# The threshold of an assignment by binary search, spread to all partitions by VectorE instead of by a matmul

## The chip, the cores and the metric

One core of a Trainium2 chip. The metric is the device time of one execution in microseconds (us): 890.03 us for the kernel before, the median of 3 runs (889.72 to 890.83).

## What is computed

Attention with a window of 128 keys, then two products with a leaky ReLU between them, then a mixture of 8 experts in which each token goes to one expert:

```python
def _moe2_ref(x, w_gate, w1, w2):
    cap = N // E
    flat = (x @ w_gate).flatten()
    order = np.argsort(-flat)
    for idx in order:
        tok, e = (int(idx) // E, int(idx) % E)
        if assigned[tok] >= 0 or counts[e] >= cap:
            continue
        assigned[tok] = e
        counts[e] += 1
    for e in range(E):
        mask = assigned == e
        out[mask] = np.maximum(x[mask] @ w1[e], 0.0) @ w2[e]
```

2304 tokens, 8 experts, 288 places each. The tokens are assigned greedily in the order of their logits over all experts. The change lies in this assignment.

## The kernel before

Products in fp32 are made of three: operands are split into a high and a low part, and high x high, high x low, low x high are summed. The high part is ScalarE's (a copy into a narrower type), the low part VectorE's (the difference).

The stages follow one another: attention with the first product (`w_in`), the second product (`w_out`, to `x2_dram`), and the experts. The second product has 18 blocks of 128 tokens, each of 48 matmuls of 512 columns into one bank `po` (line 221). It is written as a generator: `fill(n)` emits the next n of these matmuls wherever it is called. The order on every engine is the order of the code in this part.

The assignment (`assign`, line 744 on) needs the logits alone and runs beside the second product. It has 7 phases. In each, every open token names the expert that it likes best, and a search finds, for all experts at once, a threshold above which the tokens fit into the places left. The search has two calls of `search` with three rounds each, so 42 rounds in all: the first two rounds of a call try 32 values, the third 64. One round is:

- VectorE compares the keys with the values: `ge` (line 805; 128x576 for 32 values, 128x1152 for 64), and subtracts the last threshold from the keys (line 806);
- `low()` takes a low part from a list (line 808, the work at line 189): a piece of 128x512 of a block of the second product to come or of an expert's weight;
- TensorE does 6 or 9 fills (`F_GE`), then 18 small matmuls that count, per value and expert, the keys that pass: `cnt` (line 812), 32 or 64 rows;
- VectorE reads the counts (`jk`, `mx`, line 815) and tests whether they fill a place: `ok` (line 818), one number per value, on 32 or 64 partitions;
- if the list holds more than 2 pieces, a second low part (line 820);
- TensorE does 3 fills (`F_NB`) and a matmul of ones by `ok`, which sums `ok` and leaves the threshold on all 128 partitions of a PSUM bank, `nb` (line 823). The next comparison reads it as its scalar.

At the end of a phase, totals go through TensorE (`tp`, lines 741 to 871). Behind the last phase stand 22 fills, a prefix sum by TensorE (`pre`), a chain on VectorE (`t`, `w`, `W`, `U`, lines 900 to 920), 24 fills and the matmuls `ip` (line 924) that give the list of tokens of each expert. What is left in the list of low parts is done behind that (line 940), unless a block needs it: the generator calls `lows_of` ahead of a block's first and 25th matmul, which emits the missing low parts there.

A low part's second piece also issues, on SP's queue, the load that reuses its buffer (`gin`, line 201); ScalarE makes the high part of that load (`goh`, line 181).

Of the kernel before, what the change touches and what calls it, by code (L numbers as in the profile page):

```python
# [9 lines left out]
F32 = mybir.dt.float32  # L10
F32R = mybir.dt.float32r
BF16 = mybir.dt.bfloat16
# [3 lines left out]
ALU = mybir.AluOpType  # L16
AX = mybir.AxisListType.X
PSUM = bass.MemoryType.PSUM

P = 128  # L20
# [26 lines left out]
LOW_PIECES = 2  # L47
# [77 lines left out]
def tile_attn_moe_moe2(ctx: ExitStack, tc: tile.TileContext, q_in, k_in, v, w_in, w_out, w_gate, w1, w2, consts, out):  # L125
    nc = tc.nc
    V, A, T, GP = nc.vector, nc.scalar, nc.tensor, nc.gpsimd
# [9 lines left out]
    def bank(tag, name, bufs=None):  # L137
        kw = {} if bufs is None else dict(bufs=bufs)
        return ps.tile([P, 512], F32, tag=tag, name=name, **kw)
# [4 lines left out]
    def C(name):  # L144
        return cst[:, COLS[name][0]:COLS[name][1]]
# [3 lines left out]
    ones_b = cpool.tile([P, P], BF16, name="ones_b")  # L149
# [27 lines left out]
    lows = []  # L177
# [8 lines left out]
    def low(n=1):  # L186
        for _ in range(min(n, len(lows))):
            wl, cs, st, wh, then = lows.pop(0)
            V.tensor_tensor(out=wl[:, cs], in0=st[:, cs], in1=wh[:, cs].bitcast(F32), op=ALU.subtract)  # L189
            if then:  # L190
                then()
# [48 lines left out]
    def fill(n):  # L240

        nonlocal emitted
        for _ in range(n):
            emitted += next(products, 0) is None
# [56 lines left out]
    with ExitStack() as actx:  # L301
# [283 lines left out]
        if True:  # L585
# [13 lines left out]
            for c in range(H // 2):  # L599
                (V if c < BIAS_V else GP).tensor_scalar(bias_sb[:, c, :], C("rel"), C("slope")[:, c:c + 1], None,  # L600
                                                        op0=ALU.mult)
# [120 lines left out]
    def rt(shape, dt, tag, bufs=1):  # L722
        return bpool.tile(shape, dt, tag=tag, name=tag, bufs=bufs)

    def TT(o, a, b, op):
        V.tensor_tensor(out=o, in0=a, in1=b, op=op)
# [13 lines left out]
    def prefix_sum(src, acc, pre):  # L740
        T.matmul(pre, tri_b, src.rearrange("p e i -> p i e"), start=True, stop=False)
        T.matmul(pre[:, 1:], ones_b, acc[:, :, :NB - 1].rearrange("p e i -> p i e"), start=False, stop=True)

    def assign(fill):
# [5 lines left out]
                        op1=ALU.bitwise_or)  # L750
# [46 lines left out]
        def search(kt, nb, oh, weight, beside):  # L797

            for cn, n, step in (("c1", 32, 2048.0), ("c2", 32, 64.0), ("c3", 64, weight)):
                ge = rt([P, NB, n], BF16, f"ge{n}")  # L800
                k, c = kt.unsqueeze(2).to_broadcast([P, NB, n]), C(cn).unsqueeze(1).to_broadcast([P, NB, n])
                if nb is None:
                    TT(ge, k, c, ALU.is_ge)
                else:
                    V.scalar_tensor_tensor(out=ge, in0=k, scalar=nb, in1=c, op0=ALU.subtract, op1=ALU.is_ge)
                    V.tensor_scalar(kt, kt, nb, None, op0=ALU.subtract)
                beside[cn]()
                low()
                fill(F_GE[n])
                cnt = bank("t", "cnt")[:n, :NE]  # L810
                for i in range(NB):
                    T.matmul(cnt, ge[:, i, :], oh[:, i, :], start=(i == 0), stop=(i == NB - 1))  # L812
                jk = rt([P, NE], F32, "jk")
                mx = rt([P, 1], F32, "mx")
                V.tensor_tensor_reduce(out=jk[:n], in0=cnt, in1=need[:n], scale=1.0, scalar=-1e9,
                                       op0=ALU.subtract, op1=ALU.max, accum_out=mx[:n])
                ok = rt([P, 1], BF16, "ok")
                V.tensor_scalar(ok[:n], mx[:n], 0.0, step, op0=ALU.is_ge, op1=ALU.mult)
                if len(lows) > LOW_PIECES:
                    low()  # L820
                fill(F_NB)
                nb = bank("v", "nb", bufs=1)[:, :1]
                T.matmul(nb, ones_b[:n, :], ok[:n], start=True, stop=True)
            return nb

        for ph in range(NE - 1):
# [21 lines left out]
            def nothing():  # L848
                pass

            nb = search(kh, None, oh, 65536.0, dict(c1=low_key, c2=account, c3=both_keys))
            nb = search(k2, nb, oh, 1.0, dict(c1=nothing, c2=nothing, c3=nothing))

            m1, m0 = rt([P, NB], F32, "m1"), rt([P, NB], F32, "m0")
# [8 lines left out]
            with nc.allow_low_precision("counts up to 18"):  # L863
# [23 lines left out]
                                   op1=ALU.add)  # L887
# [5 lines left out]
        TT(ab, asg, oh, ALU.add)  # L893

        fill(F_PRE)
        pre = bank("l", "pre", bufs=1)[:, :NB * NE].rearrange("p (i e) -> p i e", i=NB)
        prefix_sum(ab_e, acc, pre)
        t1, t2 = rt(B3, F32, "t1"), rt(B3, F32, "t2")
# [24 lines left out]
        for i in range(NB):  # L923
            T.matmul(ip, U[:, i, :], W[:, i].rearrange("p a c -> p (a c)"), start=(i == 0),
                     stop=(i == NB - 1))
# [3 lines left out]
                               op1=ALU.add)  # L929
# [7 lines left out]
        first["hot"] = hot.rearrange("p g s -> p (g s)")  # L937

    assign(fill)
    low(len(lows))  # L940
    fill((NB - 1) * 48 + 1 - emitted)
# [172 lines left out]
```

## Time and profile before

| | |
|---|---|
| median of 3 runs | 890.03 us (889.72 to 890.83) |
| the profiled execution | 894.0 us, its span 892.2 us |
| TensorE matmuls, share of the span | 839.7 us, 94% |
| VectorE, share of the span | 523.0 us, 59% |
| ScalarE, share of the span | 394.1 us, 44% |
| matmuls of the second product (line 221) in the chain that ended last | 23% of the span |
| counts (line 812) in that chain | 3% of the span |

The chain that ended last is followed back from the last instruction to whatever released each step; 81% of it is TensorE, 8% VectorE, 5% ScalarE. The assignment lies between about 400 and 616 us of the span. A busy time is that of an engine's instructions from start to end, and neighbours on one engine can overlap.

### The profile page before, as it was taken

How to read it: one execution, taken by the hardware profiler on the slowest of the kernel's cores; microseconds unless marked ns; L12 is line 12 of the kernel's file. 1: busy time of each engine (PE TensorE's matmuls, PEld its weight loads, DVE VectorE, ACT ScalarE, POOL GpSimd, SP SyncE). 2: the span in 40 equal slices, each digit the busy share in tenths (PEclk: the TensorE clock that was granted, in tenths of full speed). 3: DMA queues.
4: the chain of work that ended last, by engine and by line, in shares of the span. 5: the costliest groups of instructions: out<-in, count | busy, mean ns of one | idle time of the engine just before them, and what ended most of it. 6: DMA issues, size and time to landing. Idle time of an engine off the chain costs nothing.

```text
span 892.2 us, 18599 instructions
## 1 busy us (share of the span) xinstructions
PE 839.7 (94%) x7590; PEld 732.4 (82%) x7590; DVE 523.0 (59%) x1311; ACT 394.1 (44%) x867; POOL 56.4 (6%) x82
## 2 busy tenths in 40 slices
PE   5578899899999999999999999998999999999995
PEld 3467889899999888877776767776889999999995
DVE  3778774767744452358778787774235555555540
ACT  6776665565655553232121212111234655556551
POOL 0000000000000000000000000000020222112211
PEclk9788899899999999999999999999999999999998
DMA  9964665765539998763324242221345665566630
GB/s 293 250 225 152 186 200 182 207 185 172 172 96 238 246 241 215 189 191 122 133 73 143 85 140 84 95 83 69 121 136 166 214 191 174 181 211 212 189 111 27
DMA packets 103638, 147.19 MB, mean 165 GB/s; under 512 B 6145, under 2 KB 74369, under 8 KB 101505
## 3 DMA queue, kind: packets, MB, share of 16 engines
q1 hardware_dynamic: 100480, 136.56, 51.2%
q0 software_dynamic: 3072, 9.44, 3.1%
q8 instruction: 60, 0.98, 0.5%
q14 instruction: 26, 0.20, 0.1%
HBM read 113.21 MB, written 32.77 MB: 164 GB/s over the span
## 4 chain that ended last, share of the span: by engine, by line
PE 81%; DVE 8%; ACT 5%; issue 4%; POOL 1%; DMA 0%; SPq 0%; POOLq 0%; ACTq 0%; DVEq 0%
PE po L221 23%; PE h L507 21%; PE m L992 11%; PE y L1011 10%; PE xv L482 3%; PE pt L465 3%; PE cnt L812 3%; PE lg L534 2%; PE s L423 2%; ACT pr L453 2%; ACT pr L441 2%; DVE dt L361 1%; PE wtp L386 1%; PE yo L1021 1%; ACT dt L343 1%
## 5 line engine op out<-in xcount | busy, mean ns | idle before, releaser
L221 PE MATMUL po<-wh_out,gol 128*128 128x512 f32 x272 | 112.0, 412 | 4.6 <-DVE gol L189 4.6
L221 PE MATMUL po<-wh_out,goh 128*128 128x512 f32 x272 | 110.6, 406 | 0.0
L221 PE MATMUL po<-wl_out,goh 128*128 128x512 f32 x272 | 110.5, 406 | 0.0
L507 PE MATMUL h<-xh,wh_in 128*128 128x256 f32 x576 | 96.7, 292 | 4.1 <-DVE gb L520 4.1
L520 DVE TENSOR_TENSOR gb<-h,th 128x512 f32<-128x512 f32 x72 | 49.7, 690 | 80.6 <-ACT th L516 77.1
L181 ACT ACTIVATE goh<-gin 128x1024 fp32r<-128x1024 f32 x34 | 36.0, 1060 | 126.9 <-DMA gin<-g_dram 120.9
L507 PE MATMUL h<-xh,wl_in 128*128 128x256 f32 x576 | 91.2, 281 | 0.0
L507 PE MATMUL h<-xl,wh_in 128*128 128x256 f32 x576 | 90.6, 280 | 0.0
L516 ACT ACTIVATE th<-h 128x512 f32<-128x512 f32 x72 | 42.7, 594 | 107.5 <-PE h L507 107.5
L158 DVE TENSOR_TENSOR wl_w<-st_w,wh_w 128x1024 fp32r<-128x1024 f32 x60 | 72.9, 1225 | 26.7 <-ACT wh_w L157 26.7
L507 PEld LDWEIGHTS h<-xh,wh_in 128*128 128x128 f32 x576 | 80.3, 196 | 9.1 <-DVE gb L520 4.5
L507 PEld LDWEIGHTS h<-xh,wl_in 128*128 128x128 f32 x576 | 78.9, 193 | 0.0
L507 PEld LDWEIGHTS h<-xl,wh_in 128*128 128x128 f32 x576 | 77.7, 190 | 0.0
L1011 PE MATMUL y<-hh,wh_w 128*128 128x288 f32 x256 | 77.4, 302 | 0.0
L1011 PE MATMUL y<-hh,wl_w 128*128 128x288 f32 x256 | 75.6, 295 | 0.0
L1011 PE MATMUL y<-hl,wh_w 128*128 128x288 f32 x256 | 75.5, 295 | 0.0
L441 ACT ACTIVATE pr<-neg,nm 128x192 f32<-128x192 f32 (+2 forms) x144 | 61.2, 428 | 29.5 <-DVE nm L438 29.2
L221 PEld LDWEIGHTS po<-wh_out,gol 128*128 128x128 f32 x272 | 51.5, 189 | 15.9 <-DVE gol L189 6.3
L157 ACT ACTIVATE wh_w<-st_w 128x1024 fp32r<-128x1024 f32 x60 | 62.5, 1053 | 2.8 <-DMA st_w<-in_w_dram 2.8
L221 PEld LDWEIGHTS po<-wl_out,goh 128*128 128x128 f32 x272 | 51.4, 189 | 10.1 <-issue 0.2
L995 DVE SCALAR_TENSOR_TENSOR hl<-m,hh 128x288 fp32r<-128x288 f32 x64 | 29.1, 455 | 51.8 <-ACT hh L994 51.8
L221 PEld LDWEIGHTS po<-wh_out,goh 128*128 128x128 f32 x272 | 51.5, 190 | 9.5
(219 smaller groups left out, 1541.0 us busy)
## 6 DMA issues: line engine op xcount, KB each, us to landing
st_w<-in_w_dram SPq DMA_DIRECT2D x64, 512.0 KB, 4.0
g_dram<-gb SPq DMA_DIRECT2D x72, 256.0 KB, 3.9
gin<-g_dram SPq DMA_DIRECT2D x34, 512.0 KB, 3.9
gr<-g_dram SPq DMA_DIRECT2D x48, 256.0 KB, 6.1
v<-in_v_dram SPq DMA_DIRECT2D x28, 384.0 KB, 5.8
raw<-in_w_in_dram SPq DMA_DIRECT2D x8, 1024.0 KB, 9.5
raw<-in_w_out_dram SPq DMA_DIRECT2D x8, 1024.0 KB, 5.4
x_dram<-xo SPq DMA_DIRECT2D x17, 256.0 KB, 2.0
```

Of the source, the lines that this page charges most:

```text
L157: A.activation(wh, st, AF.Copy)
L158: lo_engine.tensor_tensor(out=wl, in0=st, in1=wh.bitcast(F32), op=ALU.subtract)
L181: A.activation(wh, st, AF.Copy)
L221: T.matmul(po, g, w, start=(k == 0), stop=(k == 47))
L441: A.activation(pr[:, i, :nk], neg[:, a, :nk], AF.Exp, scale=-1.0, bias=nm[:, i:i + 1], accum_out=sm[:, i:i + 1])
L465: T.transpose(pt[:kn, a, kb, :], pr[:, 2 * hf + a, kb * kn:kb * kn + kn], ident)
L507: T.matmul(hp[:, j, :], w[:, d, j * P:(j + 1) * P], x[:, d, :], start=(k == 0), stop=(k == 11))
L516: A.activation(th, hp, AF.Copy, scale=0.01)
L520: V.tensor_tensor(out=gbs[c][:, o:o + 2, :], in0=hp, in1=th, op=ALU.max)
L992: T.matmul(hp, w[:, d, :], x[:, d, :], start=(k == 0), stop=(k == 11))
L995: V.scalar_tensor_tensor(out=hl[:, f, :], in0=hp, scalar=0.0, in1=hh[:, f, :].bitcast(F32), op0=ALU.max, op1=ALU.subtract)
L1011: T.matmul(yp, w, x[:, f, :], start=(k == 0), stop=(k == 23))
```

## The change

`ok` becomes a tile of 32 rows: each group of 32 thresholds tested is written as a 32x32 block in which a row holds one value 32 times (two blocks for 64 values). VectorE transposes the blocks, so that each row holds all 32 or 64 values, and sums them along the row four times, once into each group of 32 partitions of `nb`, which now lies in SBUF. The matmul is gone, the 3 fills stay. The second low part of a round moves from behind `ok` to the place of the first. Two low parts are added ahead of the prefix sum at the end (`low(LOW_PIECES)`).

```diff
--- before.py
+++ after.py
@@ -805,7 +805,7 @@
                     V.scalar_tensor_tensor(out=ge, in0=k, scalar=nb, in1=c, op0=ALU.subtract, op1=ALU.is_ge)
                     V.tensor_scalar(kt, kt, nb, None, op0=ALU.subtract)
                 beside[cn]()
-                low()
+                low(2 if len(lows) > LOW_PIECES else 1)
                 fill(F_GE[n])
                 cnt = bank("t", "cnt")[:n, :NE]
                 for i in range(NB):
@@ -814,13 +814,16 @@
                 mx = rt([P, 1], F32, "mx")
                 V.tensor_tensor_reduce(out=jk[:n], in0=cnt, in1=need[:n], scale=1.0, scalar=-1e9,
                                        op0=ALU.subtract, op1=ALU.max, accum_out=mx[:n])
-                ok = rt([P, 1], BF16, "ok")
-                V.tensor_scalar(ok[:n], mx[:n], 0.0, step, op0=ALU.is_ge, op1=ALU.mult)
-                if len(lows) > LOW_PIECES:
-                    low()
+
+                ok, tr = rt([32, 64], F32, "ok"), rt([32, 64], F32, "tr")
+                for x in range(0, n, 32):
+                    V.tensor_scalar(ok[:, x:x + 32], mx[x:x + 32].to_broadcast([32, 32]), 0.0, step,
+                                    op0=ALU.is_ge, op1=ALU.mult)
+                V.transpose(tr[:, :n], ok[:, :n])
+                nb = rt([P, 1], F32, "nb", bufs=2)
+                for x in range(0, P, 32):
+                    V.tensor_reduce(out=nb[x:x + 32], in_=tr[:, :n], op=ALU.add, axis=AX)
                 fill(F_NB)
-                nb = bank("v", "nb", bufs=1)[:, :1]
-                T.matmul(nb, ones_b[:n, :], ok[:n], start=True, stop=True)
             return nb
 
         for ph in range(NE - 1):
@@ -893,6 +896,7 @@
         TT(ab, asg, oh, ALU.add)
 
         fill(F_PRE)
+        low(LOW_PIECES)
         pre = bank("l", "pre", bufs=1)[:, :NB * NE].rearrange("p (i e) -> p i e", i=NB)
         prefix_sum(ab_e, acc, pre)
         t1, t2 = rt(B3, F32, "t1"), rt(B3, F32, "t2")
```

On VectorE the change moves low parts and puts the new instructions into each round. First the end of a round's comparison and the next threshold in the third phase (`gol` is a low part, `jk` and `mx` the counts read). Before:

```order
L189 TENSOR_TENSOR gol_0_6059<-gin_0_5892,goh_0_6058 128x512
L815 ISA jk,mx<-cnt,need 32x8
L815 ISA mx 32x1
L818 TENSOR_SCALAR ok<-mx 32x1
L189 TENSOR_TENSOR gol_0_6059<-gin_0_5892,goh_0_6058 128x512
L805 SCALAR_TENSOR_TENSOR ge_6148<-kh,nb,cst 128x576
L806 TENSOR_SCALAR kh<-kh,nb 128x18
```

And with the change, at the same place:

```order
L189 TENSOR_TENSOR gol_0_6123<-gin_0_5940,goh_0_6122 128x512 x2
L815 ISA jk,mx<-cnt,need 32x8
L815 ISA mx 32x1
L820 TENSOR_SCALAR ok<-mx 32x32
L822 STREAM_TRANSPOSE tr<-ok 32x32
L825 TENSOR_REDUCE nb<-tr 32x1 x4
L805 SCALAR_TENSOR_TENSOR ge_6217<-kh,nb,cst 128x576
L806 TENSOR_SCALAR kh<-kh,nb 128x18
```

Both low parts now stand ahead of the reading of the counts, and between `ok` and the next comparison are five instructions of VectorE.

On TensorE, the fills behind a count in the first phase (`po` is the bank of the second product):

```order
 L221 MATMUL po_5381<-wh_out_5080,gol_1_5302 128x512
 L221 MATMUL po_5381<-wh_out_5168,goh_1_5301 128x512
 L221 MATMUL po_5381<-wl_out_5169,goh_1_5301 128x512
-L823 LDWEIGHTS ones_b
-L823 MATMUL nb<-ok,ones_b 128x1
 L221 MATMUL po_5381<-wh_out_5168,gol_1_5302 128x512
 L221 MATMUL po_5381<-wh_out_5168,goh_1_5301 128x512
```

The fills on both sides of the matmul of the threshold now follow each other without a break.

On VectorE at the end of the assignment, the chain's last part before (`w`, `W` and `U` are made for the lists of tokens, `lo` reads `ip`):

```order
L909 SCALAR_TENSOR_TENSOR kh<-m_7853,kh 128x18
L726 TENSOR_TENSOR w<-kl,cst 128x432
L915 TENSOR_SCALAR W<-w,cst 128x18x24
L726 TENSOR_TENSOR W<-w,cst 128x18x24
L726 TENSOR_TENSOR U<-kh,cst 128x864 x2
L189 TENSOR_TENSOR gol_0_7820<-gin_0_7637,goh_0_7819 128x512 x2
L927 COPY lo<-ip 96x24
```

And with the change, the chain's first part (`t` reads the prefix sums `pre`):

```order
L726 TENSOR_TENSOR ab_e<-asg,oh 128x18x8
L736 SCALAR_TENSOR_TENSOR acc<-chain,ab_e 128x144
L726 TENSOR_TENSOR ab<-asg,oh 128x144
L189 TENSOR_TENSOR gol_0_8044<-gin_0_7845,goh_0_8043 128x512 x2
L726 TENSOR_TENSOR t_8073<-pre,ab 128x144
L905 TENSOR_REDUCE kh<-t_8073 128x18
```

The two low parts of the next block's first half stood behind `U` and now come ahead of `t`.

## Rows read from the trace of the kernel before

**Rows 1.** Busy time by stretch: from:to, us, busy PE, PEld, DVE, ACT, POOL, PEclk, DMA share, GB/s
```profile
412.00:597.00 185.00, 184.59 (x1406) 130.77 (x1405) 139.57 (x439) 37.35 (x41) 0.00 (x0) 1.00 0.33 108
```

**Rows 2.** List of waits, 410 to 600: us in total, times, longest us
```profile
ACT goh L181 <- DMA gin<-g_dram: 88.7, 23, 8.6
...
DVE jk L815 <- PE cnt L812: 21.0, 38, 1.3
...
DVE ge L805 <- PE nb L823: 13.7, 22, 0.7
...
DVE m L857 <- PE nb L823: 3.3, 5, 0.7
...
DVE av L726 <- PE tp L871: 2.0, 7, 0.3
```

**Rows 3.** Timeline of one round (64 rows): start us, us, engine, line, operation [idle before]
```profile
448.46 0.15 DVE L818 TENSOR_SCALAR ok<-mx 64x1 bf16<-64x1 f32 x1
448.49 0.39 PE L221 MATMUL po<-wh_out,gol 128*128 128x512 f32 x1
...
448.54 0.69 DVE L189 TENSOR_TENSOR gol<-gin,goh 128x512 fp32r<-128x512 f32 x1
448.72 0.40 PE L221 MATMUL po<-wh_out,goh 128*128 128x512 f32 x1
...
449.05 0.17 PE L823 MATMUL nb<-ok,ones_b 64*128 64x1 bf16 x1
...
449.26 0.82 DVE L805 SCALAR_TENSOR_TENSOR ge<-k,nb,cst 128x576 bf16<-128x576 f32 x1
449.49 0.40 PE L221 MATMUL po<-wh_out,gol 128*128 128x512 f32 x1
```

**Rows 4.** VectorE by line and shape, whole span: busy us, mean ns, idle before
```profile
L438 DVE DVE_READ_ACCUMULATOR2_ANT nm<- 128x1 f32 x144 | 12.0, 84 | 0.0
...
L805 DVE SCALAR_TENSOR_TENSOR ge<-k,nb,cst 128x576 bf16<-128x576 f32 x14 | 11.5, 824 | 6.3 <-PE nb L823 6.2
...
L805 DVE SCALAR_TENSOR_TENSOR ge<-k,nb,cst 128x1152 bf16<-128x1152 f32 x7 | 10.0, 1424 | 3.4 <-PE nb L823 3.3
...
L818 DVE TENSOR_SCALAR ok<-mx 32x1 bf16<-32x1 f32 x28 | 4.0, 144 | 1.0
...
L832 DVE TENSOR_REDUCE kh<-t 128x18 f32<-128x144 f32 x7 | 2.1, 303 | 0.2
...
L815 DVE DVE_READ_ACCUMULATOR2_ANT mx<- 32x1 f32 x28 | 2.0, 71 | 0.0
...
L845 DVE TENSOR_SCALAR k<-kh 128x18 f32<-128x18 f32 x7 | 1.2, 177 | 0.2
```

**Rows 5.** Timeline, VectorE at the end of a phase
```profile
434.77 0.16 DVE L726 TENSOR_TENSOR left<-av,tp 128x8 f32<-128x8 f32 x1
434.85 0.30 DVE L726 TENSOR_TENSOR tk<-tp,av 128x144 f32<-128x144 f32 x1
```

**Rows 6.** Waits of SP's queue, 410 to 600
```profile
SPq L201 <- DVE gol L189: 83.4, 20, 9.5
```

**Rows 7.** Timeline, end of the assignment, VectorE and TensorE
```profile
601.93 0.28 DVE L726 TENSOR_TENSOR ab<-asg,oh 128x144 bf16<-128x144 f32 x1
...
602.61 0.60 PE L221 MATMUL po<-wh_out,goh 128*128 128x512 f32 x1
...
603.01 0.31 DVE L726 TENSOR_TENSOR t<-pre,ab 128x144 f32<-128x144 f32 x1 [0.80 <-PE pre L742]
...
606.25 2.02 DVE L726 TENSOR_TENSOR U<-kh,cst 128x864 bf16<-128x864 f32 x2
608.18 1.28 DVE L189 TENSOR_TENSOR gol<-gin,goh 128x512 fp32r<-128x512 f32 x2
...
608.92 0.50 PE L221 MATMUL po<-wh_out,gol 128*128 128x512 f32 x1 [4.09 <-DVE gol L189]
...
614.30 0.95 PE L924 MATMUL ip<-W,U 128*96 128x48 bf16 x18
```

**Rows 8.** Busy time by stretch, behind the stall
```profile
608.90:612.50 3.60, 3.58 (x9) 2.81 (x10) 0.57 (x1) 0.00 (x0) 0.00 (x0) 0.57 0.39 139
```


## The prediction

> **What bounds the kernel now.** I read the stage of the assignment first as busy times, then its waits, then one round in order of time, then the stage's end. In the table of stretches [rows 1] TensorE is busy for 184.59 us of the 185.0 us from 412 to 597, at a granted clock of 1.00, and VectorE for 139.57. So the stage runs at TensorE's pace: between the counts stand products of the second layer ("fills"), and 42 rounds (7 phases of 6) are threaded through them. VectorE waits, and the list of waits says for what [rows 2]: 21.0 us for the counts, 13.7 and 3.3 us for the threshold's matmul, 2.0 us for the totals at the end of a phase, 40.0 us together. This idle time is the cover for anything that the change gives to VectorE, and the question is whether it is enough.
>
> **The change part by part.**
>
> *The matmul removed.* In the round in rows 3, fills stand 0.23 us apart (448.49 and 448.72). From 448.72, the last fill ahead of the threshold's matmul, to 449.49, the second behind it, are 0.77 us; without it two plain steps, 0.46. So a round gives TensorE back 0.30 us, 42 rounds 12.6 us. That is the most the removal can bring, and it comes only if VectorE has its comparison ready 0.30 us earlier in each round.
>
> *What VectorE gets instead.* Before, after the test `ok` VectorE is free 0.08 us later (448.46 to 448.54 [rows 3]) and then waits or works on a low part. Now `ok`, a transpose and four sums follow each other, and the next comparison needs the last of them. Prices, from the groups by line [rows 4]: one more column costs 1.04 ns (the comparison of 1152 columns took 1424 ns, that of 576 took 824). `ok` took 144 ns for one column; with 32 it is 0.17. A sum over 144 columns took 303 ns; over 32 it is 0.187, and I take off 0.013 for 32 partitions instead of 128 (the accumulator read took 84 ns on 128 and 71 on 32): 0.173, or 0.207 over 64. No row shows a transpose on VectorE. Below it is bounded by the shortest of these instructions with an input tile, 0.144, above by the sum over 144 columns, 0.303. I take 0.18, by the nearest row in size, the 177 ns of the 18 columns of L845. An instruction that needs the one before it starts some 0.03 after that one's end.
>
> The one choice that decides is how the four sums follow each other. They do not need each other, but each writes other 32 partitions than the one before. Rows bound it from both sides. Independent neighbours overlap: `tk` starts 0.08 us after `left`, which took 0.16 [rows 5]. So the start-to-start distance lies between the duration less 0.08 (0.093) and the whole duration and up to 0.03 more. Each overlapping pair that I found in this trace starts on the same partition as its neighbour; no row shows an overlap across different ones. So I take the whole duration, 0.173, with no gap.
>
> The Trainium skill ("VectorE: DVE Perf Modes", section "Two Vector instructions with no wait between them") says that an instruction whose output starts in another group of 32 partitions than the last one's begins only when all earlier ones have finished. By that rule the sum is the one I make here; without it, that of the first rival. No run here shows it.
>
> A round whose count has 32 rows: `ok` 0.17 + 0.03, transpose 0.18 + 0.03, sums 4 x 0.173 + 0.03, together 1.13, less the 0.08 of before: 1.05 us more. A round with 64 rows has a second `ok` (0.17, from other partitions, so also in full), 0.03 more for the transpose and 4 x 0.033 for the sums: 1.38. A phase has four of the first and two of the second kind, 6.96 us; seven phases 48.7 us. The idle time to hide this in is 40.0 less the 2.0 for the totals, which stays: 38.0 [rows 2]. **So 10.7 us do not fit, and the stage becomes that much longer, with VectorE as its bound.** TensorE's 12.6 us are then waits ahead of the counts. Behind a waiting count stand the next three fills and the six or nine behind them in TensorE's queue, so nothing else moves on.
>
> The Trainium skill (same page, section "The three transpose paths") gives 311 ns for a 128x128 bf16 transpose on VectorE; with 96 columns fewer at 0.96 GHz my estimate from that page would be 0.21 us, so 42 rounds would take 1.3 us more than with my 0.18. No run here shows it.
>
> *Low parts moved.* The second low part of a round now stands ahead of the reading of the count instead of behind `ok`. Their number is the same, 56 of 0.68 us. In place of the wait for the threshold's matmul they now lie in the wait for the counts, so the sum above, which takes all idle time as one, costs the move at nothing; if a low part comes in a round whose count is already done, it delays that round, which the following rounds without one partly take up. With a low part's second piece goes the issue of the next load on SP's queue. SP waited 83.4 us for those pieces, and ScalarE 88.7 us for the loads [rows 2, 6], and yet no wait of VectorE for ScalarE's halves is in the list; a shift by under 1 us stays hidden there.
>
> *Two low parts at the end of the stage.* This is a second gain, apart from the first. TensorE stands still for 4.09 us before 608.92, until the first low part of the next block, which VectorE begins only at 608.18, behind `U` [rows 7]. After it the granted clock is 0.57 over 3.6 us [rows 8], and the fills stand 0.43 us apart instead of 0.23. Now these two low parts run behind `ab`, whose end is 602.21, in the time in which VectorE waited 0.80 us for the prefix sums. At 0.61 us start to start they delay `t` from 603.01 to about 603.5 and the end of `U` from 608.27 to 608.8. TensorE does its 24 fills without a stop from 602.61 (24 x 0.23 + 0.2 gives 608.3), waits for `U`, and starts `ip` at 608.9 instead of 614.30: **5.4 us gained**. If the clock fell all the same, it would be 3.6.
>
> *Sum.* 10.7 longer, 5.4 shorter: 5.3 us slower. The profiled execution took 894.0 us (span 892.2 and 1.8 around it), so 899.3; it lies 4.0 us above the median of the runs, 890.03, so the forecast for the runs is 895.3 us, 0.6% slower.
>
> **The rivals.**
>
> *The sums overlap* (the other side). At 0.093 us start to start four sums take 0.48 with the last gap, in the rounds with 64 rows 0.61. A round adds 0.81 or 1.06 us, a phase 5.36, the stage 37.5: just the 38.0 that are idle. The stage keeps its length, the 5.4 us of its end stay, and the time is 884.6. The overlaps of small independent instructions in the trace speak for it; that none of them changes partitions speaks against it. It decides at 43.4 us added, half way between 37.5 and 48.7: there stage and end cancel.
>
> *The clock falls inside the stage.* With 10.7 + 12.6 us of TensorE's time now waits, in pieces of 0.1 to 1.5 us, the granted clock could drop as it did after the 4.09 us. One spell cost 3.6 us at 0.57, about 1.5 us of lost work; one per phase, as VectorE's chain at the end of each phase leaves TensorE idle, is some 7 us where half is hidden in waits already there: 902. Against it speaks that all waits of the stage before left the clock at 1.00.
>
> *The gain at the end does not come.* If VectorE reaches `ab` so late that the low parts there push `U` as far as the stall was, or the halves are not there yet, then the 5.4 us fall to about 0 while the sums overlap: 890. Little speaks for it, since the chain from `ab` to `U` keeps its length.
>
> **How the numbers follow.** Serial sums 0.52, overlapping sums 0.35, clock 0.07, no gain at the end 0.06. A measurement of this kernel can tell about 0.2% (1.8 us) from no change. Within the forecast the transpose moves the time from -1.5 (0.144) to +5.2 us (0.303), and a gap of 0.03 between the sums by +3.8 us, though hardly all together; its own range is 890 to 901. With the overlap below, the range is 884 to 901: it leaves out an overlap with cheap transposes and the clock rival. Faster: nearly all of the overlap and a little of the forecast, 0.34. Within 0.2%: the last rival, the lower edge of the forecast, some of the overlap, 0.15. Slower: 0.51.
>
> **What would show it.** If right, VectorE is busy nearly throughout from 412 to the end of the stage, and the list of waits shows TensorE waiting for the comparison and for the chain behind the threshold; the four sums start 0.17 us or more apart; the 4.09 us stall and the dip of the clock are gone, and `ip` starts within some 7 us of the prefix sums. Wrong would be sums 0.1 us apart and a stage as long as before or shorter, or a transpose much outside 0.15 to 0.30 us, or a stall before the next block's low part.

## The result, and the profile after

The changed kernel is slower: 902.29 us (median of 4 runs, 900.82 to 903.13) beside 890.43 us (889.72 to 892.25) for the kernel before on the same chip, a ratio of 1.0121 with the 95% interval [1.0105, 1.0136]. On a second chip it was 900.26 beside 890.16 us, 1.0112 [1.0097, 1.0128]. The direction is the one forecast; the loss, 11.9 us, is more than twice the 5.3 us that were forecast, and the time lies 1.3 us above the range. The profiled execution took 903.13 us, 9.1 more than the one of before.

The table of stretches, for the stage as it lies now (from:to, length, busy PE, PEld, DVE, ACT, POOL, clock, DMA share, GB/s):

```profile
412.00:612.00 200.00, 181.09 (x1358) 133.27 (x1359) 179.16 (x660) 37.34 (x41) 0.00 (x0) 0.97 0.30 98
612.20:627.00 14.80, 14.77 (x80) 11.59 (x79) 13.43 (x44) 2.72 (x3) 0.00 (x0) 1.00 0.15 54
```

Against [rows 1] the two engines have nearly changed places: TensorE, busy without a break before, now stands still for 18.9 of 200 us, and VectorE is busy for 179 where it had 139.6 of 185. The second row is the end of the stage: it runs at a granted clock of 1.00, without the stall and the low clock of [rows 7, 8]. The first row, the search, no longer does: its mean clock is 0.97.

The list of waits between 410 and 612 us (total, times, longest):

```profile
PEld L812 <- DVE ge L805: 25.1, 32, 1.8
PE cnt L812 <- DVE ge L805: 10.7, 17, 1.4
DVE jk L815 <- PE cnt L812: 7.3, 12, 1.9
```

VectorE's waits for the threshold are gone, those for the counts fell from 21.0 us [rows 2] to 7.3, and TensorE now waits for the comparisons. The 7.3 us are the row to remember: VectorE became the bound, and yet not all of its idle time was used.

The same round as in [rows 3], in the changed kernel (VectorE's timeline: start, duration, operation):

```profile
448.37 0.35 DVE L820 TENSOR_SCALAR ok<-mx 32x32 f32<-32x32 f32 x2
448.75 0.23 DVE L822 STREAM_TRANSPOSE tr<-ok 32x64 f32<-32x64 f32 x1
449.02 0.88 DVE L825 TENSOR_REDUCE nb<-tr 32x1 f32<-32x64 f32 x4
449.94 0.82 DVE L805 SCALAR_TENSOR_TENSOR ge<-k,nb,cst 128x576 bf16<-128x576 f32 x1
```

And VectorE's groups by line and shape, over the whole span (busy us, mean ns):

```profile
L825 DVE TENSOR_REDUCE nb<-tr 32x1 f32<-32x32 f32 x112 | 19.8, 176 | 2.1
L825 DVE TENSOR_REDUCE nb<-tr 32x1 f32<-32x64 f32 x56 | 11.7, 209 | 1.1
...
L820 DVE TENSOR_SCALAR ok<-mx 32x32 f32<-32x32 f32 x56 | 9.5, 169 | 1.6
L822 DVE STREAM_TRANSPOSE tr<-ok 32x32 f32<-32x32 f32 x28 | 5.6, 199 | 1.0
...
L822 DVE STREAM_TRANSPOSE tr<-ok 32x64 f32<-32x64 f32 x14 | 3.3, 232 | 0.5
```

From the test to the next comparison are 1.57 us in a round of 64 values; four sums take 0.88, so they start (0.88 - 0.21) / 3 = 0.22 us apart, a whole duration (0.209) and a little more. `ok` (169 ns) and the sums (176 and 209) came out as priced, the transposes 20 ns dearer (199 and 232).

To compare kernels I add up VectorE's timeline of the search, from the start of the first reading of a count (`jk`) to the start of the last `tk` that reads the totals. Idle is the sum of the waits shown there; what is left of the length is counted as VectorE's work, with the short gaps between instructions for which the timeline shows no wait. In us:

| kernel | length of the search | VectorE at work | waits for counts | all waits |
|---|---|---|---|---|
| before | 183.5 | 143.5 | 21.0 | 40.0 |
| the change | 199.9 | 190.3 | 7.3 | 9.6 |
| the change, low parts in one place only | 196.5 | 189.4 | 4.3 | 7.1 |
| the change, two sums in the rounds of 32 | 192.5 | 185.3 | 5.2 | 7.2 |
| the change, clock held up | 197.1 | 190.6 | 4.3 | 6.6 |
| VectorE's sums in 20 rounds only | 178.3 | 160.2 | 10.8 | 18.1 |

The two lengths run between these rows, before

```profile
414.16 0.15 DVE L815 CUSTOM_DVE_ANT_0 jk<-cnt,need 32x8 f32<-32x8 f32 x1
...
597.70 0.30 DVE L726 TENSOR_TENSOR tk<-tp,av 128x144 f32<-128x144 f32 x1
...
615.29 0.18 DVE L927 COPY lo<-ip 96x24 f32<-96x24 f32 x1 [5.82 <-PE ip L924]
```

and, with the change, from the following row to the first row of the next list:

```profile
412.65 0.15 DVE L815 CUSTOM_DVE_ANT_0 jk<-cnt,need 32x8 f32<-32x8 f32 x1
```

The end of the stage gains. These are the rows of VectorE behind the last phase:

```profile
612.56 0.30 DVE L726 TENSOR_TENSOR tk<-tp,av 128x144 f32<-128x144 f32 x1
...
617.00 1.29 DVE L189 TENSOR_TENSOR gol<-gin,goh 128x512 fp32r<-128x512 f32 x2
618.20 0.30 DVE L726 TENSOR_TENSOR t<-pre,ab 128x144 f32<-128x144 f32 x1
...
621.42 2.02 DVE L726 TENSOR_TENSOR U<-kh,cst 128x864 bf16<-128x864 f32 x2
624.26 0.18 DVE L931 COPY lo<-ip 96x24 f32<-96x24 f32 x1 [0.81 <-PE ip L928]
```

From the last `tk` to `lo` are 11.7 us; before it was 17.6 (597.70 to 615.29). So 5.9 us are gained here and 16.4 lost in the search. Their difference of 10.5, less 1.5 by which this execution happened to reach the search earlier (first count read at 412.65 instead of 414.16), is the 9.0 between the two spans.

### The profile page after: what moved, and what is told of

Its sections match the earlier page's. It is cut to its first block, busy times and chain, and to the rows that moved or that the text cites. A ratio compares the mean times of both kernels' runs of the same rounds, so it can differ in the third digit from the quotient of the medians.

```text
span 901.2 us, 18741 instructions
## 1 busy us (share of the span) xinstructions
PE 835.1 (93%) x7548; PEld 734.4 (81%) x7548; DVE 563.7 (63%) x1535; ACT 393.8 (44%) x867; POOL 56.3 (6%) x82
## 4 chain that ended last, share of the span: by engine, by line
PE 66%; DVE 21%; ACT 5%; issue 5%; DMA 1%; POOL 1%; SPq 0%; POOLq 0%; ACTq 0%; DVEq 0%
PE h L507 20%; PE m L996 10%; PE y L1015 10%; PE po L221 10%; DVE ge L805 4%; DVE nb L825 3%; DVE gol L189 3%; PE xv L482 3%; PE pt L465 3%; PE lg L534 2%; PE s L423 2%; ACT pr L441 2%; ACT pr L453 1%; PE cnt L812 1%; DMA v<-in_v_dram 1%
## 5 line engine op out<-in xcount | busy, mean ns | idle before, releaser
L221 PEld LDWEIGHTS po<-wh_out,goh 128*128 128x128 f32 x272 | 52.5, 193 | 10.8
```

The lines of the kernel that those rows point to most:

```text
L221: T.matmul(po, g, w, start=(k == 0), stop=(k == 47))
```

## The experiments

The theory after the result: the forecast's mechanism holds (serial sums fill VectorE beyond its idle time, the end gains), and the missing 5 us are idle time that could not be used. The rivals: the end gained less than thought, the sums cost more than their rows say, or the clock fell inside the stage.

**The end alone.** The kernel before with the one line `low(LOW_PIECES)` of the change.

```diff
         fill(F_PRE)
+        low(LOW_PIECES)
```

> The kernel before with one line of the change alone: two low parts ahead of the prefix sum at the end. In the change's trace the restart of the fills (behind the last totals) to the restart at full pace behind the token lists took 13.94 us (612.24 to 626.18), before 19.98 (597.23 to 617.21). My theory, that the two low parts alone removed the 4.09 us stall and the dip of the clock behind it: 6.0 us faster than before, 884.4, granted clock 1.00 throughout that stretch. Rival, that the stall went because VectorE's queue came otherwise into the end of the stage (the low parts were fewer there in any case): no more than 1 us.

Measured: 884.32 us (883.02 to 884.99), ratio 0.9926 [0.9898, 0.9953]. VectorE's timeline at that place:

```profile
594.30 0.30 DVE L726 TENSOR_TENSOR tk<-tp,av 128x144 f32<-128x144 f32 x1
...
598.72 1.28 DVE L189 TENSOR_TENSOR gol<-gin,goh 128x512 fp32r<-128x512 f32 x2
599.93 0.30 DVE L726 TENSOR_TENSOR t<-pre,ab 128x144 f32<-128x144 f32 x1
...
606.04 0.18 DVE L928 COPY lo<-ip 96x24 f32<-96x24 f32 x1 [0.87 <-PE ip L925]
```

The search is as long as before (183.5), and from the last `tk` (594.30) to `lo` are 11.7 us. This is the 6 us that were expected. The gain is shown alone, and it does not depend on the rest of the change.

**The change without that line.**

```diff
         fill(F_PRE)
-        low(LOW_PIECES)
```

> The change without the two low parts at the end. My theory: the search alone costs 16.4 us (first reading of a count to the last totals: 183.5 us before, 199.9 with the change), and the stall of some 4 us with its clock dip is back: 890.4 + 16.4 = 907, 4 to 7 us slower than the whole change. Rival: the two lines hang together and the end keeps its gain, 902.

Measured: 906.62 us (906.32 to 908.98), ratio 1.0188 [1.0158, 1.0218]. The stretch behind the assignment shows the old stall and the low clock again:

```profile
616.00:628.00 12.00, 7.92 (x42) 6.07 (x41) 6.03 (x16) 1.66 (x2) 0.00 (x0) 0.86 0.19 66
```

From `tk` (610.22) to `lo` (627.80) are 17.6 us, as before, and the time is the 907 us that were expected. So the change is two independent ones: the threshold on VectorE, which costs 1.9%, and two moved low parts, which give back 0.7%. The first rival has fallen; the missing time is in the search.

**What a sum costs, by the partitions it writes.** Two kernels add three sums that nobody reads behind the four, once all into the 32 partitions that the fourth wrote, once each into others.

```diff
                     V.tensor_reduce(out=nb[x:x + 32], in_=tr[:, :n], op=ALU.add, axis=AX)
+                dm = rt([P, 4], F32, "dm", bufs=2)
+                for x in range(3):
+                    V.tensor_reduce(out=dm[96:, x:x + 1], in_=tr[:, :n], op=ALU.add, axis=AX)
```

> The change with three more sums in each round, that nobody reads, behind the four, into the same 32 partitions as the fourth sum, in other columns. My theory, that the four sums do not overlap because each writes other partitions than the one before: these three start about 0.09 us after one another (0.13 with 64 columns), and add 0.3 to 0.4 us per round, some 12 to 15 us in all. Rival, that sums of this kind never overlap, whatever they write: they start 0.18 us apart (0.22), and add some 23 us or more.

In the other kernel the last line is:

```diff
+                    V.tensor_reduce(out=dm[32 * x:32 * x + 32, x:x + 1], in_=tr[:, :n], op=ALU.add, axis=AX)
```

> The twin of e4_same: three more sums per round that nobody reads, behind the four, but each into other 32 partitions than the one before. In e4_same they started 0.09 us apart and cost 0.29 us a round (0.42 with 64 columns), 17.7 us with what they took from the fourth sum, less 4.7; the search took 210.9 us. My theory (no overlap where the partitions of the output change): they start 0.18 us apart (0.22), the search takes some 222 us and the execution some 10 us more than e4_same, about 922. Rival (in e4_same they overlapped because nobody waits for them, whatever the partitions): 0.09 us apart and the time of e4_same.

Measured in one run each: 911.8 and 932.2 us. VectorE's timeline of the first kernel, in a round of 32 values:

```profile
441.77 0.75 DVE L825 TENSOR_REDUCE nb<-tr 32x1 f32<-32x32 f32 x4
442.44 0.35 DVE L828 TENSOR_REDUCE dm<-tr 32x1 f32<-32x32 f32 x3
```

And of the second:

```profile
444.37 0.75 DVE L825 TENSOR_REDUCE nb<-tr 32x1 f32<-32x32 f32 x4
445.14 0.55 DVE L828 TENSOR_REDUCE dm<-tr 32x1 f32<-32x32 f32 x3
```

The three sums, of the same size and the same input, take 0.35 us in the first and 0.55 in the second. With 0.17 or 0.18 for one, they start 0.09 us apart where the partitions stay, and 0.19 where they change. The choice on which the prediction turned was right, and its first rival (0.093 apart) is what these kernels show only where all write the same 32 partitions. In total time both expectations missed: the first kernel is 9.5 us above the change, not 12 to 15, and the second kernel lost 10 us more than was expected of it: its waits for counts rose to 11.7 us, and its clock was far from 1.00 in the search.

```profile
412.00:636.00 224.00, 184.84 (x1324) 136.95 (x1325) 197.02 (x760) 35.45 (x40) 0.00 (x0) 0.92 0.25 83
```

This suggests that a slow VectorE costs more than its own time, through TensorE's clock; it is tested below.

**Low parts in one place.** The change with one low part ahead of each count's reading instead of up to two; those that are left run later.

```diff
-                low(2 if len(lows) > LOW_PIECES else 1)
+                low()
```

> The change, with never more than one low part per round ahead of the reading of the count (instead of two where the list is long). In the change 7.3 us of VectorE's idle time for counts were left, which my sum had filled. My theory, that they were left because low parts come in pairs in some rounds and not at all in others: with one per round more rounds have one, the waits for counts fall by some 3 us or more and the time by 2 to 4 us, to about 899. Rival, that where the low parts stand is indifferent since VectorE is the bound with or without: within 1 us of 902. Against both: a low part that comes too late stalls a block, and the time goes up.

Measured: 898.21 us (897.61 to 899.50), ratio 1.0091 [1.0063, 1.0118], 4 us under the change's first time and 2 under its second. The search is 3.4 us shorter: the waits for counts are 3.0 us less, while 13.2 us instead of 11.7 lie between `tk` and `lo` behind it, where three low parts stand now. As expected in size; but the profile shows the low clock for some 10 us in all here and for 13.6 in the change, so this run does not tell whether the low parts' place or the clock does it.

**Two sums instead of four.** In the 28 rounds of 32 values the test is written to two groups of partitions, the transpose has 64 rows, and two sums over 64 partitions spread it.

```diff
...
+                    ok, tr = rt([64, 32], F32, "ok2"), rt([64, 32], F32, "tr2")
+                    for x in (0, 32):
+                        V.tensor_scalar(ok[x:x + 32], mx[:32].to_broadcast([32, 32]), 0.0, step,
+                                        op0=ALU.is_ge, op1=ALU.mult)
+                    V.transpose(tr, ok)
+                    nb = rt([P, 1], F32, "nb", bufs=2)
+                    for x in (0, 64):
+                        V.tensor_reduce(out=nb[x:x + 64], in_=tr, op=ALU.add, axis=AX)
```

> The change with two sums in place of four in the 28 rounds of 32 values: the test is written into two groups of 32 partitions (one more test), the transpose covers 64 partitions, and each sum covers 64. The 14 rounds of 64 values stay. VectorE's sequence behind a count gets shorter by two sums of 0.185 us and longer by one test of 0.17, 0.2 us in 28 rounds, 5.6 us. My theory, VectorE bounds the search and each microsecond that it is spared counts, less what returns as waits: 4 to 5.6 us faster than the change, 897 to 898. Rival, that the search is bound by the chain through the counts and VectorE's total does not matter: the chain is shorter by the same 0.2 us, so the same gain, but then the waits for counts do not grow; a third, that a sum over 64 partitions is no cheaper than two over 32: no gain.

Measured: 895.84 us (892.12 to 896.57, 10 runs), ratio 1.0036 [1.0021, 1.0052].

```profile
479.19 0.35 DVE L830 TENSOR_SCALAR ok<-mx 32x32 f32<-32x32 f32 x2
479.58 0.20 DVE L832 STREAM_TRANSPOSE tr<-ok 64x32 f32<-64x32 f32 x1
479.82 0.37 DVE L835 TENSOR_REDUCE nb<-tr 64x1 f32<-64x32 f32 x2
```

A sum over 64 partitions costs what one over 32 costs, so the spread takes 0.37 us instead of 0.75, a second `ok` 0.18 more. VectorE's work in the search fell by 5.1 us and the search by 7.4, more than the 4 to 5.6 us that were expected; the profile shows the low clock for 6.8 us here, half of the change's, so not all of the 7.4 need be the sums'. Fewer sums that follow each other make the threshold cheaper, but the kernel is still slower than before.

**Is it the clock?** In the change's profile the granted clock falls to 0.50 (1.2 of 2.4 GHz) four times between 480 and 577 us, for about 3.4 us each time. The table of stretches of the change, first the four stretches of 10 us that hold the dips:

```profile
480.00:490.00 10.00, 9.63 (x80) 7.28 (x81) 8.94 (x31) 0.60 (x1) 0.00 (x0) 0.83 0.22 78
520.00:530.00 10.00, 9.11 (x49) 6.77 (x49) 7.55 (x27) 1.06 (x1) 0.00 (x0) 0.83 0.22 77
540.00:550.00 10.00, 9.91 (x83) 7.16 (x81) 8.68 (x31) 1.06 (x1) 0.00 (x0) 0.86 0.52 178
570.00:580.00 10.00, 8.61 (x77) 6.24 (x75) 8.14 (x28) 2.35 (x3) 0.00 (x0) 0.83 0.40 133
...
479.00:480.00 1.00, 0.00 (x0) 0.00 (x0) 0.94 (x4) 0.00 (x0) 0.00 (x0) 1.00 0.83 258
480.00:481.00 1.00, 0.63 (x19) 0.60 (x19) 0.96 (x3) 0.00 (x0) 0.00 (x0) 1.00 0.58 234
481.00:482.00 1.00, 1.00 (x4) 0.76 (x5) 0.88 (x7) 0.00 (x0) 0.00 (x0) 0.68 0.01 4
482.00:483.00 1.00, 1.00 (x4) 0.81 (x3) 0.94 (x4) 0.00 (x0) 0.00 (x0) 0.50 0.00 0
```

The last four rows are the beginning of the first dip, us by us. And TensorE's timeline around it (start, duration, operation, what it waited for):

```profile
475.98 0.73 PE L812 MATMUL cnt<-oh,ge 128*64 128x8 bf16 x18 [0.81 <-DVE ge L805]
...
477.44 0.40 PE L221 MATMUL po<-wh_out,goh 128*128 128x512 f32 x1
477.68 0.39 PE L221 MATMUL po<-wl_out,goh 128*128 128x512 f32 x1
...
480.37 0.61 PE L812 MATMUL cnt<-oh,ge 128*32 128x8 bf16 x18 [1.39 <-DVE ge L805]
...
482.42 0.63 PE L221 MATMUL po<-wl_out,goh 128*128 128x512 f32 x1
482.85 0.63 PE L221 MATMUL po<-wh_out,gol 128*128 128x512 f32 x1
...
520.80 0.41 PE L741 MATMUL tp<-at__6852,tri_b 128*128 128x144 bf16 x1 [1.17 <-DVE at__6852 L726]
...
539.28 0.72 PE L221 MATMUL po<-wh_out,gol 128*128 128x512 f32 x1 [1.34 <-DVE gol L189]
```

TensorE waited 0.81 and 1.39 us for VectorE's comparisons, and behind that its fills stand 0.43 us apart instead of 0.24. The count behind them is late, and VectorE waits 0.55 us for it at 485.35. The last two rows show the waits ahead of the next two dips: 1.17 us at the end of a phase, and 1.34 us of a fill for a low part, the third of four that VectorE does there ahead of the reading of one count. The fourth dip again follows a comparison (1.39 us, at 571.76). Of the 7.3 us of waits for counts, 4.3 lie in such a dip or up to 4.4 us behind it (0.55, 1.94, 0.34, 0.53 and 0.96). Whether the dips cause them was tested by holding the clock up: matmuls that nobody reads, put into TensorE's own waits.

```diff
+    seen, wide = [], rt([P, 512], BF16, "wide")
+    GP.memset(wide, 1.0)
+
+    def keep(m):
+        for _ in range(m):
+            T.matmul(bank("v", "nb", bufs=1), ones_b, wide, start=True, stop=True)
...
                 fill(F_GE[n])
+                keep({3: 5, 10: 3, 14: 3, 15: 5, 21: 3, 26: 3, 33: 5, 40: 3}.get(len(seen), 0))
+                seen.append(0)
...
+                keep(5 if len(seen) == 27 else 0)
                 fill(F_NB)
...
             fill(F_TOT)
+            keep(4 if ph in (2, 3) else 2)
```

> The change, with matmuls that nobody reads (ones times ones, 128x128 by 512 columns, into the bank that the threshold no longer uses) put at the places where TensorE of the changed kernel waited longest for VectorE: 3 or 5 ahead of the counts of eight rounds (waits of 0.7 to 1.4 us), 5 ahead of one fill, 2 or 4 ahead of the totals of each phase. At 0.23 us each they should lie inside those waits; VectorE's work stays the same. In the changed kernel the granted clock fell to 0.50 four times between 480 and 577 us, each time for about 3.4 us and each time behind waits of 0.8 to 1.4 us. Theory (the dips make a good part of the 7.3 us that VectorE still waits for counts: the waits that lie in or just behind a dip are 0.55, 1.94, 0.34, 0.53 and 0.96 us, together 4.3): the dips are gone or fewer, the waits for counts fall to 3 to 4 us, the search takes about 196 us and the kernel 898 to 899 us. Rival (the dips are covered by TensorE's spare time, and the waits come from rounds without a low part): the clock is 1.00, but the waits for counts stay near 7 us, the search stays at 200 us and the time at 902. If the extra matmuls delay counts themselves, the time is above 902.

Measured: 900.13 us (899.67 to 901.39), ratio 1.0107 [1.0087, 1.0127], between the theory's 898 to 899 and the rival's 902. In the profiled run the clock was 1.00 throughout the search, and the five waits at dips were gone or smaller (together 1.3 us instead of 4.3), but at four rounds with extra matmuls VectorE waited 1.5 us longer: these counts the matmuls delayed themselves. So with fewer at those four rounds:

```diff
-                keep({3: 5, 10: 3, 14: 3, 15: 5, 21: 3, 26: 3, 33: 5, 40: 3}.get(len(seen), 0))
+                keep({3: 3, 10: 3, 14: 3, 15: 3, 21: 2, 26: 3, 33: 3, 40: 3}.get(len(seen), 0))
```

> As the last one, with 3 unread matmuls instead of 5 ahead of three counts and 2 instead of 3 ahead of a fourth: in the last run VectorE waited 0.35, 0.54 and 0.33 us at those counts and 0.25 more at the fourth, which it does not in the changed kernel, so the extra matmuls themselves delayed them. Theory (the dips of the clock make 3.0 us of the 7.3 us of waits for counts, of which the last run's own matmuls gave back 1.5): with the clock at 1.00 the waits for counts are 4.2 to 4.5 us, the search takes 197 to 198 us, the kernel 898.5 to 899.5, 3 us under the change as it stands, run beside it on the same chip. Rival (the dips cost nothing that TensorE's spare time does not cover): within 1 us of the change as it stands. If too few matmuls are left, the dips come back and nothing is told apart.

> The changed kernel as it stands, for its time on the same chip as the run beside it: 901 to 903 us and a ratio near 1.012.

Measured on one chip: 898.47 us (897.90 to 899.71), ratio 1.0089 [1.0075, 1.0102], and the change as it stands 900.26 (899.08 to 900.62), ratio 1.0112 [1.0097, 1.0128], 0.7 us less than was expected of it. The stretch of the search and the wait for counts, first with the clock held up:

```profile
412.00:608.00 196.00, 188.18 (x1385) 132.16 (x1385) 178.09 (x657) 36.92 (x41) 0.00 (x0) 1.00 0.30 99
```

```profile
DVE jk L824 <- PE cnt L821: 4.3, 9, 0.8
```

And the change as it stands, beside it:

```profile
412.00:608.00 196.00, 176.28 (x1323) 129.45 (x1320) 176.37 (x648) 35.58 (x40) 0.00 (x0) 0.97 0.30 97
```

```profile
DVE jk L815 <- PE cnt L812: 6.7, 12, 1.2
```

More matmuls, and a shorter time, though not the 3 us that were expected. VectorE's work is the same (190.6 and 190.3 us); the search is 2.1 us shorter, and the waits for counts are 2.3 us less. The medians differ by 1.8 us, with intervals that overlap a little; the traces say which way and where. So the dips cost 2 to 3 us of this kernel (2.3 beside the run on the same chip, 3.0 beside the first profile). The rest, 4.3 us, stays at full clock: 2.9 in six of the nine rounds that have no low part, 1.35 in the first rounds of three phases. Of the 1.94 and 0.96 us above, 0.76 and 0.55 are among it: they stay with the clock at 1.00, so only part of those two waits was the dips'.

**A version that beats both.** The end's line, and the threshold on VectorE only where it was idle anyway: in rounds of 32 values that no longer have two low parts waiting (20 of 42), with two sums; elsewhere the matmul as before.

```diff
+                here = n == 32 and len(lows) <= LOW_PIECES
...
+                if here:
...
+                    fill(F_NB)
+                    continue
```

> e1_tail, with the threshold spread by VectorE (two sums, as in e7_two) only in the rounds of 32 values in whose place not more than one low part is due, 20 of 42; the matmul and the second low part stay in the others. My theory: VectorE has 40 us of waits in the search of e1_tail; 20 rounds with some 0.95 us more each take 19 of it, so TensorE stays the bound and gets its 0.30 us back in each, less short waits where a round's low part makes the next comparison late: 2 to 6 us faster than e1_tail, 878 to 882. Rival: what a round gains, the next one loses, since VectorE comes late into it: the time of e1_tail, 884.

Measured: 879.52 us (878.15 to 881.34), ratio 0.9869 [0.9846, 0.9892]. The search, in the table of stretches, and the longest of VectorE's waits in it:

```profile
407.00:590.00 183.00, 182.28 (x1401) 133.03 (x1400) 156.03 (x534) 38.42 (x42) 0.00 (x0) 1.00 0.34 110
```

```profile
DVE jk L816 <- PE cnt L813: 10.8, 22, 1.0
```

TensorE stays busy and the clock at 1.00, and the search is 5.2 us shorter than before. Twenty matmuls of 0.30 us would be 6.0: here nearly all of the removal's gain comes. VectorE still waits for 18.1 us, so TensorE remained the bound.

## Why the prediction was right in direction and wrong in size

Its steps in order.

*The matmul removed: right.* It was priced at no gain unless VectorE is ready earlier. In the change it gave nothing; in the last experiment 5.2 of 6.0 us for 20 rounds.

*What VectorE gets: right within 5%.* Forecast 48.7 us. In the trace, start to start, the sums took 34.7, the transposes 10.3, and `ok` 6.0 more than before, 51.0 together: 2.3 too little was forecast, mostly for sums 0.19 instead of 0.173 apart. The low parts gave 3.7 back, which the prediction did not have: 50 of the 56, where it was 11 before, are now followed by an instruction that starts before the low part's end. VectorE's work grew by 46.8.

*The sums do not overlap: right*, and shown by the pair of experiments. The rule of the Trainium skill that the prediction cited ("VectorE: DVE Perf Modes", section "Two Vector instructions with no wait between them": another group of 32 partitions waits for all earlier instructions) now has this case's numbers beside it, 0.19 us where the group changes and 0.09 where it does not.

*"... the sum above, which takes all idle time as one, costs the move at nothing", and with it "the idle time to hide this in is ... 38.0": this step failed.* Only 30.4 us (40.0 less 9.6) were filled. The idle time lay in 42 rounds, and work was added to every round alike. In six of the nine rounds without a low part TensorE stayed the slower one, while rounds with two low parts and the new chain became longer than TensorE's part, so that TensorE waited up to 1.4 us; what one round lacked, another could not lend. At full clock 4.3 us of waits for counts stay. The trace of before allows an estimate: if each round fills no more than its own idle time (the wait for its threshold and that for the next count, or, counted the other way, for its own count) with its 1.05 or 1.38 us, 32 or 36 us are filled, not 38.0. That moving the second low part ahead of the reading adds to it was argued, and the run with one place agrees in size, but it had fewer dips too; that share stays open. The prediction saw that a low part "in a round whose count is already done" delays that round, and counted on the following rounds to take it up; in the round at 539.28 the counts were done at 537.51 and read at 539.75, behind four low parts.

*"The clock falls inside the stage", a rival at 0.07, came true in part.* Its price was 7 us with one spell in each of seven phases; there were four spells of some 3.4 us at 0.50, worth 2 to 3 us by the runs that held the clock up. That its time, 902, is the one measured is luck: it has 7 us where the clock cost 2 to 3, and seven spells of 1.5 us, half of them hidden, would by its own figures be 5.3. The reason against it ("all waits of the stage before left the clock at 1.00") compared with a stage in which TensorE hardly waited, and could not speak for one in which it does.

Together: the search was to be 10.7 us longer and was 16.4 longer, which is 1.9 less work on VectorE than forecast and 7.6 of idle time that was to be filled and was not: 2 to 3 of it by the clock's dips, the rest, as far as the traces tell, by where the idle time lay. The range had bounds for the transpose and for the gaps between the sums, and none for this term; its lower edge, 890, follows from none of the bounds named, of which the cheapest transpose gives 893.8.

*The end of the stage: right.* 5.9 us for the forecast 5.4, shown alone.

*From the profile to the runs.* The forecast took 4.0 us off, by which the profiled execution lay above the median. The change's lies 0.8 above its own. By the profiles the forecast of 899.3 was 3.8 low, by the runs of 895.3 it was 7.0 low; the difference is where an execution stands among its kind before the stage (the first count was read anywhere between 409.2 and 414.2 us in the profiles of this study), which one execution cannot tell.

## What to carry to other kernels

Cover is counted where it lies: before a wait's total is used as room for new work, split it by round, and take for each round the lesser of its wait and the work that it gets. When another engine becomes the bound, TensorE's new waits have a price of their own: look at the longest single wait that the plan makes, and at the granted clock behind it. And a change of two parts is run as two: here a line that gains 0.7% was hidden in one that loses 1.9%, and the first, together with the second in 20 of the 42 rounds only, beats both kernels.

## What was not expected of the hardware

The clock's dips come and go between executions of one program. Ahead of the count of the same round (at 422.86 and 419.56 us) TensorE waited 1.38 us in both profiles of the change; in the first the clock stayed at 1.00 behind it, in the second it fell to 0.50. So a wait of that length need not bring a dip. Where TensorE was kept busy, by unread matmuls or by leaving the threshold of 22 rounds to its own matmul, the profiles show 1.00 throughout the search.

A sum over 64 partitions takes no longer than one over 32 (179 and 176 ns for 32 columns), and a transpose of 64x32 no longer than one of 32x32 (203 and 199 ns), while 32 more columns cost 33 ns: on VectorE the rows were free here, the columns and the number of instructions were not.
